# Gated linear attention with causal experts on one core: scores from split operands, the first half batch by chunks, a compact state, eight PSUM banks and a hinted branch

## The chip, the cores and the metric

The kernel runs on 1 core of a Trainium2 chip. The metric is the device time in microseconds (us); before the change the median of 3 runs is 330.34 us (329.6 to 331.68). An execution taken by the profiler took 328.62 us, and its span, from the first to the last instruction, is 326.9 us. The engines are named as in the profile: PE is TensorE, PEld its weight loads, DVE is VectorE, ACT is ScalarE, POOL is GpSimd, SP is SyncE, which issues every DMA.

## What is computed

A linear attention with a decaying state gives y, and y goes through four causal attention heads ("experts") of which each token takes two.

```python
for t in range(S):                       # B, H, S, D = 4, 8, 768, 48
    state = alpha[:, :, t, :, None] * state + np.einsum('bhd,bhe->bhde', k[:, :, t], v[:, :, t])
    y[:, :, t] = np.einsum('bhd,bhde->bhe', q[:, :, t], state)
...
logits = x @ w_gate                      # x: y with the heads side by side, 768 x 384 for each batch
... w: softmax of the two largest logits of a token, 0 for the others
for e in range(E):                       # 4 experts, 64 wide
    q, k, v = x @ wq[e], x @ wk[e], x @ wv[e]
    scores = np.where(causal, -1e9, scale * (q @ k.transpose(0, 2, 1)))
    a = softmax(scores)
    out += w[e] * (a @ v @ wo[e])
```

## The kernel before

**Units and chunks.** The time axis is cut into 24 chunks of 128 tokens (6 for each of 4 batches). Three chunks make a unit, a half batch, of which there are 8. A chunk's linear attention ("gla") does this: `prep_r` and `prep_c` (L417, L442) run two scans over alpha on DVE and scale q and k with the results; `gla_a` (L474) forms k times q on PE into two PSUM tiles, which go to SBUF masked (one by DVE, L489; the other by ACT and then POOL, L492 and L496); `gla_t` transposes k (L507); `gla_u` (L516) multiplies k by v for the state, and brings the state S forward (the decay at a chunk's end is `ev`) in two halves, on DVE (L544) and then POOL (L547); `gla_y` (L571) forms y, which is split into a rounded part `xh` (ACT, L581) and the remainder `xl` (DVE, L585). `check` squares the scans into `acc` (L471), from which the end of the kernel learns whether the scans stayed in range.

**A unit's experts.** `front(u)` makes the projections of a whole unit: `proj` (L604) nine products xh·wh, xl·wh, xh·wl of 384 columns for q and k of each of two pairs of experts, `vproj` (L622) the same with 260 columns for v and the gate, and `gate` on DVE. q and k come out in plain fp32 (ACT, L609 and L612). `back(u)` then runs, for each pair and each of the unit's three row blocks i, `score` (two fp32 products q·k, one for each expert of the pair, on rows 0 to 63 and 64 to 127 of the array, L679; DVE adds the causal mask and takes the row's extreme in one instruction, L687; ACT takes the exponential, L696), `norm` (two small DVE instructions L708 and L709, then POOL scales the row block, L715), `transp` (PE transposes L733, ACT copies L747), `av` (L770) and `outp` (L796, ACT L801, and the DMA to the output, L803).

**What sets the order.** The program is written as steps (`op` of class `Plan`, L82) with an engine, costs and the tiles they read and write; `schedule` (L122) plays them through these costs and picks, for each engine, the step that can start first, and among those within 0.05 us the one that was written first. The result is a fixed order for each engine. `emit` issues it, and wherever the plan leaves PE idle for over 0.45 us in the first 45 us it adds filler products (`warm`, L979) into an eighth PSUM bank of their own; the plan has the other seven (`GB = 7`). How far units and chunks run ahead of each other is set by the `mix` weights. The first unit starts like this: three chunks one after the other, then the splits of the weights into a rounded part and a remainder (`wqk_l`, `wv_l`, `wo_l`), then `front(0)`.

**The end.** After the last step DVE counts the flags in `acc`, PE sums them (L989), DVE writes the sum `cnt` (L991), each engine loads it into a register (L992) and compares (L993): if any scan left its range, a long exact program runs, otherwise the engines jump over it to the end.

## Time and profile before

| what | value |
|---|---|
| median of 3 runs | 330.34 us |
| profiled execution, and its span | 328.62 us, 326.9 us |
| PE busy in the span | 317.0 us (97%) |
| DVE busy | 239.7 us (73%) |
| ACT busy | 214.3 us (66%) |
| POOL busy | 134.3 us (41%) |
| DMA read and written | 24.44 MB, 4.72 MB |

A PE matmul of fp32 operands is recorded as two passes, so 128 score products are 256 records. Matmuls overlap: a record's length holds the way through the array too, and what one costs in a stream is the distance to the next one's start. On DVE and ACT likewise each record is some 0.08 to 0.1 us longer than the distance between starts.

### The profile page before, as it was taken

Reading aid. Unit: us, or ns where it says so; the run is one execution under the profiler, and the core shown is the slowest. Engines: PE = TensorE matmul, PEld = TensorE weight load, DVE = VectorE, ACT = ScalarE, POOL = GpSimd, SP = SyncE. Lnnn points to the kernel's source line nnn. Section 1 sums busy time; section 2 is a strip of 40 time slices with the busy share of each in tenths; the row PEclk is TensorE's granted clock in tenths of the full one; section 3 lists DMA queues with packets and bytes.
Section 4 is the critical chain, followed back from the end, with each engine's and each line's share of the span. In section 5 each row is a group of like instructions: output and inputs, shape, how many; then the busy total and the mean of one; then the engine's idle time right before and its main releaser. Section 6 shows DMA issues by size and latency. Waiting matters only on the chain.

```text
span 326.9 us, 9547 instructions
## 1 busy us (share of the span) xinstructions
PE 317.0 (97%) x3715; PEld 265.0 (81%) x3715; DVE 239.7 (73%) x692; ACT 214.3 (66%) x543; POOL 134.3 (41%) x190
## 2 busy tenths in 40 slices
PE   8999999999999999999999999999999999999991
PEld 6879988879797897988888687988978786957690
DVE  6899999899999999989797780939359155195420
ACT  1464586759875595756659296856837658569750
POOL 4142267434473366814349071615315324236310
PEclk9999999999999999999999999999999999999996
DMA  6999355144323253234240610412000000100101
GB/s 193 281 269 244 88 145 154 30 135 145 106 83 111 72 164 116 93 100 121 59 138 26 172 37 1 119 50 88 0 26 26 26 0 2 49 27 7 67 24 60
DMA packets 13797, 29.85 MB, mean 91 GB/s; under 512 B 1616, under 2 KB 4912, under 8 KB 13744
## 3 DMA queue, kind: packets, MB, share of 16 engines
q1 hardware_dynamic: 13744, 29.16, 31.1%
q8 instruction: 31, 0.51, 0.7%
q14 instruction: 22, 0.18, 0.2%
HBM read 24.44 MB, written 4.72 MB: 89 GB/s over the span
## 4 chain that ended last, share of the span: by engine, by line
PE 92%; DVE 4%; POOL 1%; ACT 1%; issue 0%; POOLq 0%; ACTq 0%; DVEq 0%
PE g L604 15%; PE g L679 11%; PE g L571 11%; PE g L733 11%; PE g L770 10%; PE g L796 8%; PE g L622 8%; PE g L480 7%; PE pw L979 5%; PE g L525 3%; PE g L507 2%; DVE a L687 1%; POOL a L715 1%; DVE al L451 0%; DVE qk L455 0%
## 5 line engine op out<-in xcount | busy, mean ns | idle before, releaser
L715 POOL TENSOR_SCALAR a<-a,cf,gw 128x128 f32<-128x128 f32 (+5 forms) x96 | 88.7, 936 | 62.9 <-DVE cf L709 43.1
L696 ACT ACTIVATE a<-a,mx 128x128 f32<-128x128 f32 (+5 forms) x96 | 63.3, 662 | 17.6 <-DVE mx L687 17.4
L687 DVE CUSTOM_DVE_ANT_0 a<-g,cm 128x384 f32<-128x384 f32 (+3 forms) x96 | 47.1, 529 | 5.1 <-PE g L679 4.8
L747 ACT ACTIVATE at<-g 128x512 f32<-128x512 f32 (+3 forms) x124 | 48.4, 465 | 0.9 <-PE g L733 0.7
L733 PE MATMUL g<-ident,a 128*128 128x128 f32 x336 | 46.3, 275 | 0.5 <-DVE mx L687 0.2
L679 PE MATMUL g<-k,q 64*128 64x256 f32 (+3 forms) x256 | 43.8, 454 | 0.0
L733 PEld LDWEIGHTS g<-ident,a 128*128 128x128 f32 x336 | 38.1, 141 | 5.2 <-POOL a L715 2.3
L770 PE MATMUL g<-at,vg 128*64 128x384 f32 (+2 forms) x324 | 39.5, 391 | 0.0
L770 PEld LDWEIGHTS g<-at,vg 128*64 128x64 f32 x324 | 20.9, 137 | 18.3 <-issue 14.4
L547 POOL TENSOR_TENSOR S<-st,ev 48x192 f32<-48x192 f32 x32 | 20.4, 637 | 36.1 <-DVE st L544 35.1
L604 PE MATMUL g<-xh,wqk_h 128*128 128x384 f32 x96 | 34.4, 358 | 0.1
L571 PE MATMUL g<-ms,vt 128*32 128x128 f32 x768 | 33.2, 275 | 0.1
L604 PE MATMUL g<-xl,wqk_h 128*128 128x384 f32 x96 | 32.4, 338 | 0.0
L604 PE MATMUL g<-xh,wqk_l 128*128 128x384 f32 x96 | 32.4, 338 | 0.0
L428 DVE TENSOR_TENSOR_SCAN al<-al,d1r 112x516 f32<-112x516 f32 (+1 forms) x25 | 30.2, 1212 | 2.4 <-DMA al<-in_al_dram 2.4
L679 PEld LDWEIGHTS g<-k,q 64*128 64x128 f32 x256 | 23.9, 186 | 9.4 <-issue 4.7
L451 DVE TENSOR_TENSOR_SCAN al<-al,d1c 112x516 f32<-112x516 f32 (+1 forms) x25 | 30.6, 1223 | 0.5
L496 POOL TENSOR_SCALAR_AFFINE_SELECT ms<-ms 128x512 f32<-128x512 f32 x24 | 16.2, 675 | 33.2 <-ACT ms L492 32.6
L471 ACT ACTIVATE al<-al 112x1033 f32<-112x1033 f32 x24 | 25.8, 1075 | 1.7 <-DVE qk L459 1.2
L480 PEld LDWEIGHTS g<-qk 48*128 48x128 f32 x384 | 24.2, 187 | 3.2 <-issue 1.2
L480 PE MATMUL g<-qk 48*128 48x128 f32 x384 | 26.2, 278 | 0.0
L571 PEld LDWEIGHTS g<-ms,vt 128*32 128x32 f32 x768 | 20.6, 109 | 5.3 <-issue 2.3
(91 smaller groups left out, 624.2 us busy)
## 6 DMA issues: line engine op xcount, KB each, us to landing
qk<-in_qk_dram SPq DMA_DIRECT2D x23, 448.0 KB, 4.3
vt<-in_v_dram SPq DMA_DIRECT2D x24, 256.0 KB, 4.4
al<-in_al_dram SPq DMA_DIRECT2D x23, 226.2 KB, 2.7
out_dram<-ot SPq DMA_DIRECT2D x24, 192.0 KB, 1.9
at<-in_wqk_dram SPq DMA_DIRECT2D x1, 768.0 KB, 11.1
qk<-in_qk_dram SPq DMA_DIRECT2D x2, 224.0 KB, 3.2
at<-in_wvg_dram SPq DMA_DIRECT2D x1, 390.0 KB, 10.6
at<-in_wo_dram SPq DMA_DIRECT2D x1, 384.0 KB, 12.7
```

The costliest lines, as they stand in the source:

```text
L428: V.tensor_tensor_scan(backwards(al[0:P, AW + c0 - 1:AW + c1 - 1]), backwards(al[0:P, c0:c1]), d1r[0:P, sl].rearrange("p a w -> p (a w)"), ...
L451: V.tensor_tensor_scan(c, c, T(("d1c", n))[0:P, sl].rearrange("p a w -> p (a w)"), 0.0, OP.mult, OP.max)
L480: PE.matmul(T(("pa", n, s))[:, C * p:C * p + C], t[r:r + D, p, C:2 * C], t[r:r + D, p, 0:C], start=True, stop=True, tile_position=(r, 0))
L571: PE.matmul(py[32 * j:32 * j + 32, k], l, r, start=(i == 0), stop=(i == len(parts) - 1), tile_position=(0, 32 * j))
L604: PE.matmul(pj[:, :W3], w[:, kt, cs], x[:, kt, :], start=(i == 0), stop=(i == 8))
L679: PE.matmul(T(sk[e])[:, :w], q[r, ts], k[r, c0:c1], start=True, stop=True, tile_position=(64 * e, 0))
L687: V.tensor_tensor_reduce(T(ak[e])[:, c0:c1], T(sk[e])[:, :w], cm[:, m0:m0 + w], -1.0, mx[:, 0:1] if x else BIG, OP.add, OP.min, accum_out= ...
L696: A.activation(a[:, 0:n], a[:, 0:n], AF.Exp, bias=T(mk)[:, e, len(pieces) - 1:len(pieces)], scale=-1.0, accum_out=T(("sm", u))[:, ix:ix + 1])
L715: G.tensor_scalar(a[:, 0:n], a[:, 0:n], T(ck_)[:, e:e + 1], T(("gw", u))[:, i, eg:eg + 1], op0=OP.mult, op1=OP.mult)
L733: PE.transpose(pt[:, 128 * (j - j0):128 * (j - j0) + 128], a[:, 128 * j:128 * j + 128], ident)
L747: A.activation(dst, src, AF.Copy)
L770: PE.matmul(py[64 * e:64 * e + 64, lo:n1], v[:, j % 3, 64 * eg:64 * eg + 64], at[e][:, at_off(j) + lo:at_off(j) + n1], start=(j == 0), sto ...
```

## The change

- **Scores.** q and k are kept split, like x: a rounded part (ACT) and the remainder (a DVE subtraction, new: `split`), both of type fp32r, which PE takes in one pass. A score is then three products, q1·k1 + q1·k2 + q2·k1, for each of the two experts, in alternation.
- **First unit.** `projp` makes q and k of unit 0 for one chunk at a time, 18 products of 128 columns for a pair; `vproj` follows each chunk; the splits of the weights stand ahead of chunk 1; scores of pair 0 start after each chunk. SP's first loads are ordered anew, the weights ahead of v of chunk 1. The chunk numbered 5 is loaded twice, once by the new loop and once by `chunk(3)`.
- **State.** The state is kept as C, 112 partitions x 192; one DVE and one POOL instruction bring it forward in place of two and two; ACT copies both halves into S (two new instructions a chunk, 40 in all).
- **Chunks 0 to 2** have both masked tiles made by ACT and POOL, not DVE. One d1c buffer in place of two; three buffers for q (twice the size) in place of four.
- **Eight banks.** The plan has all eight PSUM banks; fillers go to the eighth until the plan first takes it.
- **Order.** A table of 552 turns (`TURN`) replaces "written first" as the choice among steps that could start about together.
- **The end.** The count of flags (`verdict`) is a step ahead of the last unit; each engine gets a branch prefetch hint some 9 us before the planned end; the range test of the loaded value is left out.

```diff
-DMA_RATE = 220.0
+DMA_RATE = 250.0
...
-GB = 7
-MS_DVE = 0
+GB = 8
+HINT = 9.0
+TURN = (
+    5, 17, 3, 30, 13, 72, 1, 4, 117, 15, 6, 154, 142, 59, 65, 61, 8, 93, 84, 223, 180, 68, 56, 97, 123, 29, 52, 102,
...
+MS_ACT = 3
...
-                        t, i = min(c, key=lambda x: x[1])
+                        t, i = min(c, key=lambda x: rank[x[1]])
...
+                warming = warming and all(self.slot_of[k] != GB - 1 for k in o["new"] if self.kinds[k[0]] == "g")
...
-                if o["start"] < WARM_UNTIL and gap > WARM_GAP:
+                if warming and gap > WARM_GAP:
...
-        "q": slots("q", 4, [128, W3]),
-        "k": slots("k", 3, [128, S]),
+        "q": slots("q", QB, [128, 2, W3], F32R),
+        "k": slots("k", 3, [128, 2, S], F32R),
...
+            if c == 0:
+                op("V", 0.36, 0.37, lambda T: V.tensor_tensor(T(("C", n + 1))[0:P], pu(T), e(T), OP.mult),
+                   r=whole(("pu", n)) + ev, w=whole(("C", n + 1)))
+            else:
+                op("V", 0.36, 0.37, lambda T: V.tensor_tensor(T(("C", n + 1))[0:P], pu(T), T(("C", n))[0:P], OP.add),
+                   r=whole(("pu", n), ("C", n)), w=whole(("C", n + 1)))
+                op("G", 0.52, 0.53, lambda T: G.tensor_tensor(T(("C", n + 1))[0:P], T(("C", n + 1))[0:P], e(T), OP.mult),
+                   r=ev, w=whole(("C", n + 1)))
...
+                op("A", 0.21, 0.3, lambda T, rows=rows, cols=cols: A.activation(
+                    T(("S", n + 1))[rows, :, cols], T(("C", n + 1))[rows], AF.Copy),
+                   r=whole(("C", n + 1), ("S0",)), w=[(("S", n + 1), s)])
...
+        def split(src, c0, n, key, d0, part):
+            cs, ds = slice(c0, c0 + n), slice(d0, d0 + n)
+            op("A", *act(n), lambda T: A.activation(T(key)[:, 0, ds], T(src)[:, cs], AF.Copy),
+               r=whole(src), w=[(key, (0, part))])
+            op("V", *vec(n), lambda T: V.tensor_tensor(T(key)[:, 1, ds], T(src)[:, cs], T(key)[:, 0, ds].bitcast(F32),
+                                                       OP.subtract),
+               r=[(src, None), (key, (0, part))], w=[(key, (1, part))])
...
-                    for e in (0, 1):
-                        r = slice(64 * e, 64 * e + 64)
-                        PE.matmul(T(sk[e])[:, :w], q[r, ts], k[r, c0:c1], start=True, stop=True,
-                                  tile_position=(64 * e, 0))
-                occ = 2 * (0.008 + w / 1200)
...
+                    for m, (x, y) in enumerate(((0, 0), (0, 1), (1, 0))):
+                        for e in (0, 1):
+                            r = slice(64 * e, 64 * e + 64)
+                            PE.matmul(T(sk[e])[:, :w], q[r, x, ts], k[r, y, c0:c1], start=(m == 0), stop=(m == 2),
+                                      tile_position=(64 * e, 0))
+                occ = 3 * (0.013 + w / 2400 if w > 128 else N128)
...
+                for which in (0, 1):
+                    col = slice(256 * which + 128 * pair, 256 * which + 128 * pair + 128)
+                    m = 0
+                    for kt in range(3):
+                        for w, x in ((wqk_h, xh), (wqk_h, xl), (wqk_l, xh)):
+                            PE.matmul(pj[:, 128 * which:128 * which + 128], w[:, kt, col], x[:, kt, cs],
+                                      start=(m == 0), stop=(m == 8))
...
+            vproj(0, n)
...
+            for pair in (0, 1):
+                projp(0, pair, n)
+            if n:
+                score(0, 0, n - 1)
+            loads(n + 3)
...
+    for e, x in ((PE, "PE"), (V, "V"), (A, "A"), (G, "G"), (SY, "S")):
+        with tc.issue_after(pl.anchor[x].ins):
+            tc.mark_branch_hint_location("exact", "LikelyTaken", [e.engine])
```

What the new order does is seen on three queues. First PE, around the first score; before (L480 is `gla_a`, L679 the scores of q and k, g are PSUM banks):

```order
L480 MATMUL g_69<-qk_74 128x128
L679 MATMUL g_65<-k_104,q_100 128x128
L679 MATMUL g_64<-k_104,q_100 128x128
L679 MATMUL g_68<-k_104,q_100 128x256
L679 MATMUL g_67<-k_104,q_100 128x256
L679 MATMUL g_66<-k_104,q_100 128x384
L679 MATMUL g_69<-k_104,q_100 128x384
L571 MATMUL g_63<-ms_91,vt_81 32x128 x4
```

and now (L869 is `projp`, L555 `gla_t` of chunk 2, L730 the scores):

```order
L869 MATMUL g_67<-xh_96,wqk_h 128x128
L869 MATMUL g_67<-xl_98,wqk_h 128x128
L869 MATMUL g_67<-xh_96,wqk_l 128x128
L555 MATMUL g_66<-ident,qk_77 128x112 x4
L730 MATMUL g_68<-k_103,q_100 128x128
L730 MATMUL g_69<-k_103,q_100 128x128
L730 MATMUL g_68<-k_103,q_100 128x128
L730 MATMUL g_69<-k_103,q_100 128x128
L730 MATMUL g_68<-k_103,q_100 128x128
L730 MATMUL g_69<-k_103,q_100 128x128
L528 MATMUL g_70<-qk_77 128x128
```

A score of one width is now six products into two banks, in turns, where it was two; and the first one stands ahead of `gla_a` of chunk 2, where it stood behind that of chunks 3 and 4.

Second, DVE in the start; before, from chunk 2's second scan on (L455 and L459 scale k and q, al is alpha, at holds the unsplit weights):

```order
L451 SCALAR_TENSOR_TENSOR al_2_72<-al_2_72,d1c_0_86 112x516
L455 TENSOR_TENSOR qk_2_76<-qk_2_76,al_2_72 112x4x128
L459 TENSOR_TENSOR qk_2_76<-qk_2_76,al_2_72 112x4x128
L373 SCALAR_TENSOR_TENSOR wqk_l_155<-at_0_137,wqk_h_154 128x3x256
L585 TENSOR_TENSOR xl_0_98<-g_1_64,xh_0_96 128x3x128
L377 TENSOR_TENSOR wqk_l_155<-at_0_137,wqk_h_154 128x3x256
L489 TENSOR_TENSOR ms_0_90<-g_4_67,mask_149 128x512
L544 TENSOR_TENSOR st_1_93<-g_0_63,S_1_95 48x192
L428 SCALAR_TENSOR_TENSOR al_3_73<-al_3_73,d1r_147 112x516
L544 TENSOR_TENSOR st_1_93<-g_0_63,S_1_95 48x192
L432 RECIPROCAL d1c_1_87<-al_3_73 112x4
L381 TENSOR_TENSOR wv_l_157<-at_1_138,wv_h_156 128x780
```

and now (L662 is the remainder of q or k):

```order
L471 RECIPROCAL d1c_0_87<-al_2_73 112x4
L421 TENSOR_TENSOR wv_l_158<-at_1_137,wv_h_157 128x780
L490 SCALAR_TENSOR_TENSOR al_2_73<-al_2_73,d1c_0_87 112x516
L413 SCALAR_TENSOR_TENSOR wqk_l_156<-at_0_136,wqk_h_155 128x3x256
L633 TENSOR_TENSOR xl_0_98<-g_7_70,xh_0_96 128x3x128
L588 TENSOR_TENSOR C_1_93<-g_0_63,C_0_92 112x192
L417 TENSOR_TENSOR wqk_l_156<-at_0_136,wqk_h_155 128x3x256
L424 TENSOR_TENSOR wo_l_160<-at_1_137,wo_h_159 128x768
L494 TENSOR_TENSOR qk_2_77<-qk_2_77,al_2_73 112x4x128
L498 TENSOR_TENSOR qk_2_77<-qk_2_77,al_2_73 112x4x128
L662 TENSOR_TENSOR q_0_100<-g_2_65,q_0_100 128x128
L662 TENSOR_TENSOR k_0_103<-g_2_65,k_0_103 128x128
```

The remainders of the weights moved ahead of chunk 2's scaling, the masked tile of chunk 2 left this queue, and the remainders of q and k came into it.

Third, SP at the end; before (ISA x2 is the range test):

```order
L803 DMA out_0_dram<-ot_0_145 128x384
L803 DMA out_0_dram<-ot_1_146 128x384
L992 TENSOR_LOAD cnt_3889
L992 ISA x2
L993 COMPARE_AND_BRANCH
```

and now:

```order
L1186 BRANCH_PREFETCH_HINT
L856 DMA out_0_dram<-ot_1_145 128x384
L856 DMA out_0_dram<-ot_0_144 128x384
L856 DMA out_0_dram<-ot_1_145 128x384
L1087 TENSOR_LOAD cnt_153
L1088 COMPARE_AND_BRANCH
```

The range test is gone, and the hint stands three output DMAs ahead of the branch; PE, DVE, ACT and POOL have one too.

## Rows read from the trace of the kernel before

**Rows 1.** The page: the span, the busy time of the engines with its share and the count of instructions, and two lines of the 40 slices (busy tenths of DVE, granted clock of PE in tenths).

```profile
span 326.9 us, 9547 instructions
PE 317.0 (97%) x3715; PEld 265.0 (81%) x3715; DVE 239.7 (73%) x692; ACT 214.3 (66%) x543; POOL 134.3 (41%) x190
DVE  6899999899999999989797780939359155195420
PEclk9999999999999999999999999999999999999996
```

**Rows 2.** Busy time by stretch of the span (from:to, its length, then busy us and instructions of PE, PEld, DVE, ACT and POOL, granted clock, DMA share, GB/s).

```profile
27.20:45.40 18.20, 18.20 (x261) 16.93 (x262) 17.33 (x46) 10.75 (x27) 4.54 (x9) 1.00 0.50 121
45.40:138.50 93.10, 92.67 (x1154) 79.81 (x1155) 88.93 (x227) 68.18 (x178) 52.84 (x63) 1.00 0.39 116
138.50:319.50 181.00, 180.38 (x1935) 147.34 (x1933) 110.61 (x381) 122.76 (x319) 67.22 (x92) 1.00 0.18 53
319.50:326.90 7.40, 0.08 (x2) 0.00 (x0) 0.14 (x1) 0.49 (x1) 0.00 (x0) 0.66 0.20 66
```

**Rows 3.** The chain that ended last, in order of time (start, length, what): the end of the start.

```profile
25.65 1.52 PE pw L979 x13
27.18 1.09 PE g L622 x9
```

**Rows 4.** Groups of instructions by line and shape (records, then busy us, mean ns of one, idle time ahead of them): the scores by width, products in the one-pass type, fillers, and weight loads of 128 and 32 columns.

```profile
L679 PE MATMUL g<-k,q 64*128 64x512 f32 x64 | 17.5, 604 | 0.0
L679 PE MATMUL g<-k,q 64*128 64x256 f32 x96 | 15.5, 389 | 0.0
L679 PE MATMUL g<-k,q 64*128 64x384 f32 x64 | 13.9, 492 | 0.0
L679 PE MATMUL g<-k,q 64*128 64x128 f32 x32 | 3.5, 274 | 0.0
L604 PE MATMUL g<-xh,wqk_l 128*128 128x384 f32 x96 | 32.4, 338 | 0.0
L979 PE MATMUL pw<-d1r 128*128 128x256 bf16 x117 | 15.9, 290 | 1.6 <-POOL d1r L388 1.6
L604 PEld LDWEIGHTS g<-xh,wqk_l 128*128 128x128 f32 x96 | 18.0, 188 | 0.0
L571 PEld LDWEIGHTS g<-ms,vt 128*32 128x32 f32 x768 | 20.6, 109 | 5.3 <-issue 2.3 <-DVE mx L687 1.7 <-DVE cf L709 0.3
```

**Rows 5.** PE in order of time (start, length, count): a score of 512 columns and what follows it; one of 128 columns and what follows it; two one-pass products of 260 columns; two of 384.

```profile
246.42 1.03 PE L679 MATMUL g<-k,q 64*128 64x512 f32 x4
247.28 1.06 PE L480 MATMUL g<-qk 48*128 48x128 f32 x16
...
130.92 0.39 PE L679 MATMUL g<-k,q 64*128 64x128 f32 x4
131.15 1.06 PE L480 MATMUL g<-qk 48*128 48x128 f32 x16
...
27.62 0.28 PE L622 MATMUL g<-wv_h,xl 128*128 128x260 f32 x1
27.74 0.28 PE L622 MATMUL g<-wv_h,xh 128*128 128x260 f32 x1
...
300.59 0.34 PE L796 MATMUL g<-wo_h,yh 128*128 128x384 f32 x1
300.77 0.34 PE L796 MATMUL g<-wo_l,yh 128*128 128x384 f32 x1
```

**Rows 6.** The start in order of time: the first scan, then the remainders of the weights on DVE, and ACT's rounding of wqk.

```profile
3.03 0.70 DVE L428 TENSOR_TENSOR_SCAN al<-al,d1r 112x258 f32<-112x258 f32 x1 [1.01 <-DMA al<-in_al_dram]
...
17.63 0.84 ACT L364 ACTIVATE wqk_h<-at 128x768 fp32r<-128x768 f32 x1 [0.67 <-DMA at<-in_wqk_dram]
...
22.30 0.95 DVE L377 TENSOR_TENSOR wqk_l<-at,wqk_h 128x768 fp32r<-128x768 f32 x1
...
33.24 0.67 DVE L455 TENSOR_TENSOR qk<-qk,al 112x512 f32<-112x512 f32 x1
33.82 0.69 DVE L459 TENSOR_TENSOR qk<-qk,al 112x512 f32<-112x512 f32 x1
```

**Rows 7.** Groups by line and shape, as in rows 4, of DVE: remainders of 384 and of 128 columns, and the state.

```profile
L585 DVE TENSOR_TENSOR xl<-g,xh 128x384 fp32r<-128x384 f32 x24 | 13.2, 549 | 10.4 <-ACT xh L581 10.2
L544 DVE TENSOR_TENSOR st<-g,S 48x192 f32<-48x192 f32 x32 | 11.3, 353 | 5.2 <-PE g L525 3.9 <-POOL S L547 0.4 <-ACT at L747 0.4
L781 DVE TENSOR_TENSOR yl<-g,yh 128x128 fp32r<-128x128 f32 x3 | 0.9, 292 | 2.3 <-ACT yh L779 2.2
```

**Rows 8.** The end: the last output DMAs, and the sequencers' instructions of two lines (count, shortest/median/longest ns, first and last start).

```profile
319.01 1.38 SPq L803 DMA_DIRECT2D out_dram<-ot  x2
...
L993 SPq EVENT_SEMAPHORE  x8: 17/17/17, 324.4 to 324.9; - x8
...
L993 PEldq COMPARE_BRANCH  x1: 4322/4322/4322, 320.6 to 320.6; - x1
L993 SPq COMPARE_BRANCH  x1: 45/45/45, 321.3 to 321.3; - x1
...
L1091 SPq EVENT_SEMAPHORE  x10: 17/28/28, 325.0 to 326.8; - x10
```

**Rows 9.** The page's list of DMA issues (count, KB each, median us from issue to landing): the output.

```profile
out_dram<-ot SPq DMA_DIRECT2D x24, 192.0 KB, 1.9
```

More of the change, by code (lines that the diff above doesn't have):

```diff
@@ L245, in emit @@
             if warm is not None and o["eng"] == "PE":
+                warming = warming and all(self.slot_of[k] != GB - 1 for k in o["new"] if self.kinds[k[0]] == "g")
                 gap = o["start"] - pe
[L247 removed]
+                if warming and gap > WARM_GAP:
                     warm(int(gap / WARM_MM * 0.8))
                 pe = o["start"] + o["occ"]
[L250 removed]
+            x = o["fn"](self.tile)
+            if x is not None and o["start"] < self.end - HINT:
+                self.anchor[o["eng"]] = x
 @with_exitstack
@@ L472, in check, with verdict, f @@
             op("A", 1.05, 1.15, f, r=whole(("acc",)), w=whole(("al", n)) + whole(("acc", n)))
+        def verdict():
+            def f(T):
+                V.tensor_scalar(okm[0:P, 1:], acc[0:P], SAFE, None, op0=OP.is_le)
+                V.tensor_reduce(okm[0:P, 0:1], okm[0:P, 1:], axis=AX.X, op=OP.add)
+            op("V", 0.25, 0.3, f, r=whole(*[("acc", n) for n in range(NG)]), w=whole(("okm",)))
+            op("PE", 0.05, 0.2, lambda T: PE.matmul(T(("pk", 0))[0:1, 0:1], okm[0:P, 0:1], ones[0:P], start=True, stop=True),
+               pe="pk", r=whole(("okm",), ("lm",)), w=whole(("pk", 0)))
+            op("V", 0.09, 0.15, lambda T: V.tensor_copy(cnt, T(("pk", 0))[0:1, 0:1]), r=whole(("pk", 0)), w=whole(("cnt",)))
         def gla_a(n):
@@ L816, in front, with back @@
                     yield
-        def back(u):
+        def back(u, made=0):
             tail = u == NU - 1
@@ L823, in back @@
                 if k < len(seq):
-                    score(u, *seq[k])
+                    if k >= made:
+                        score(u, *seq[k])
                     norm(u, *seq[k])
@@ L896, in build @@
         constants()
+        load_al(1)
         load_v(0)
-        load_al(1)
         load_q(1)
+        wload(1)
         constants2()
         load_v(1)
-        for p in (0, 2):
-            prep_r(0, p, 2)
-            prep_c(0, p, 2)
-        loads(2)
-        gla_a(0)
-        gla_t(0)
-        check(0)
-        wload(0)
-        gla_y(0)
-        run(chunk(1))
-        wload(1)
-        constants3()
-        run(chunk(2))
-        split_hi(0)
-        split_lo(0)
-        split_lo(1)
-        split_hi(1)
-        split_lo(2)
+        load_al(2)
+        wload(0)
+        load_q(2)
+        load_v(2)
+        for n in range(HALF):
+            if n == 0:
+                for p in (0, 2):
+                    prep_r(0, p, 2)
+                    prep_c(0, p, 2)
+            else:
+                prep_r(n)
+                gla_u(n - 1)
+                prep_c(n)
+            gla_a(n)
+            gla_t(n)
+            gla_y(n)
+            if n == 0:
+                split_hi(1)
+                split_lo(2)
+            vproj(0, n)
+            if n == 0:
+                split_hi(0)
+                split_lo(0)
+                split_lo(1)
+                constants3()
+            for pair in (0, 1):
[3 more added lines that the diff above has]
+            loads(n + 3)
+        check(0)
+        check(1)
+        check(2)
         split_lo(3)
         half = lambda h: gla(h) if h < NU else None
-        b, g = chain(front(0), back(0)), half(1)
+        gate(0)
+        b, g = back(0, 2), half(1)
         mix((b, MIX_BACK0), (g, MIX_GLA0), until=g)
```

137 lines of the change are left out of this document (71 added, 66 removed), and 23 rows, old and new, of the table TURN.

## The prediction

> **What bounds the kernel now.** I read the page first: PE is busy 97% of the span; DVE's slices are at 8 and 9 through the first half and lower after it [rows 1]. Then the chain in order of time: it runs through fillers up to the first v product of the experts at 27.18 us [rows 3]. There are 117 fillers [rows 4]; at 256 columns, 0.12 us each by the products of 260 columns [rows 5], they are some 13 us of work that no result needs. Then the stretches after it [rows 2]. From 27.2 to 138.5 us PE is full (110.9 of 111.3 us) and DVE nearly so: 17.3 of 18.2 us, then 88.9 of 93.1 us [rows 2]. From 138.5 to 319.5 us PE alone is full, and DVE works 110.6 of 181 us. The last 7.4 us hold no work at all. The clock is granted in full throughout [rows 1]. So a saving on PE counts where DVE does not hold it up, DVE's own additions are nearly free after 138.5 us and not before, and the empty end counts in full.
>
> **Scores.** A score of 512 columns (both experts) takes 0.86 us of PE's queue, start to next start, and one of 128 takes 0.23 us [rows 5]; in between I go in a straight line: 0.44 and 0.65 us for 256 and 384. By the records (four for each score of two experts) there are 8, 24, 16 and 16 scores of 128, 256, 384 and 512 columns [rows 4]: 8 x 0.23 + 24 x 0.44 + 16 x 0.65 + 16 x 0.86 = 36.6 us. Now each is three steps of two one-pass products. A one-pass product costs 0.12 us at 260 columns and 0.18 at 384 [rows 5], that is its columns at 2.4 GHz plus 0.013 us: 0.226, 0.173 and 0.120 us at 512, 384 and 256. Do the two experts' products run side by side? No one-pass products on half the array stand in this trace. The two-pass ones do run so: a record of 512 columns lasts 604 ns, against 338 ns for 384 one-pass columns, of which 160 are columns and 178 the way through [rows 4]; 604 - 178 = 426 ns, and four such start within 860 ns [rows 5], so two run at a time. I take the same for one pass. A step of 128 columns would cost 0.066 us by its columns; but each product loads 128 columns of weights. Loads last 188 ns for 128 columns and 109 for 32 [rows 4], so 0.82 ns a column, 105 ns for 128, and I see no product here that was shorter than its load. I take 0.105 for it, which is nearer to what was seen, and keep 0.066 for the range. Sum: 8 x 0.32 + 24 x 0.36 + 16 x 0.52 + 16 x 0.68 = 30.4 us. **Scores: -6.2 us** (-7.2 with narrow steps at 0.066).
>
> The Trainium skill, "TensorE: Matmul & The Clock Gate", section "Back-to-back issue gap", gives 81 ns for a product of 128 columns in a stream of loads and products, between my two values; no run here shows it. By it the narrow steps below would cost 2.6 us less than in my sum.
>
> **The start.** Before, the projections waited for wqk_l, whose second half DVE began at 22.30 us [rows 6]. Now it stands ahead of chunk 2's scaling. Adding DVE's new queue from its first scan at 3.03 us [rows 6] with the start-to-start distances (0.6 us for 512 columns, as 33.24 to 33.82 [rows 6], hence about 0.08 less than each record's length; 1.15 for a scan): chunk 0 4.8 us, chunk 1 and its state 5.0, chunk 2's scans with wv_l, wqk_l, the first xl and C 4.9, and about 1 us of waits, as before: wqk_l is done at 18.7 us and not 23.2. The weights come from DMA earlier (they pass v of chunk 1 on SP's queue), so ACT's rounding, at 17.63 us before, isn't late. The first q and k products start 8.2 us sooner than at 26.9 and, with the v product made before them (1.1 us), PE is ahead by 9.3; but work that before lay ahead of them now lies behind: y of chunks 1 and 2 and the rest of chunk 2, 4.5 us. Left: 4.8. Against it, q and k of unit 0 are 108 products of 128 columns at 0.105 = 11.3 us in place of 36 at 0.176 = 6.3: +5.0 (+0.8 at 0.066). And PE waits for DVE in between, since the remainder of chunk 1's x stands behind two scans of chunk 3: about 1 us (3.5 if the narrow products are short, since then the wait is only longer). **Start: +1 us** (-0.5 to +2.5). The 54 fillers fewer are no gain beyond this. Two things cost nothing by my reading: the second load of chunk 5 (0.93 MB) goes where the DMA share falls to 0.5 and less [rows 2], and the one d1c buffer, written by the DVE instruction just ahead of its reader. Without cover the load would be 3.5 us of a full DMA queue, ahead of chunk 6.
>
> **VectorE.** Added: 12 remainders of 128 and 28 of 384 columns, 0.21 and 0.47 us (records of 292 and 549 ns [rows 7] less 0.08). Removed: half of the 40 state instructions (0.28 us each, record 353), three masked tiles (0.6), one memset. Over the kernel +8 us, most of it late where DVE has 70 us free. Before the end of unit 1 (138.5 us) it is 12 x 0.21 + 12 x 0.47 - 8 x 0.28 - 2 x 0.6 - 0.5 = +4.3 us, where 4.2 us were free [rows 2]. Some of it will reach PE, some fills waits: **+1.5 us** (0 to +5.5). ACT gets 40 copies into S of about 0.25 us and three masked tiles, 12 us on an engine with 112 us free; POOL loses 16 state instructions.
>
> **Order and banks.** PE shows no idle time to take after 27.2 us [rows 2]; what a new order and an eighth bank can take are waits too short to show as idle, inside the matmuls' overlap. Changes between row, column and full tiling are as many as before (76 and 78 along PE's order). I put a small gain here: **-1 us** (0 to -4).
>
> **The end.** The last two output DMAs are issued from 319.0 to 320.4 us. SP then loads and tests cnt, branches at 321.3, and only at 324.4 executes the next instruction; PE's branch lasts 4.32 us [rows 8]. These are waits for the target's code, which no engine holds. From 324.4 to the end at 326.8 SP's two strings of semaphore instructions and the last barrier take 2.4 us [rows 8]. If the hint brings the code, SP stands at its branch some 0.6 us after its last issue, at 321.0, and starts the strings there; the last output lands 1.9 us after its issue at 320.1 [rows 9], about 322.0, in the midst of the first string, and what is left of the 2.4 us ends about 323.8. **-3.0 us**; without an effect of the hint only the test goes, -0.4.
>
> **Sum:** 326.9 - 6.2 + 1 + 1.5 - 1 - 3.0 = 319.2 us of span. The profiled execution had 1.7 us around its span, which makes 320.9; its 328.62 us lie 1.7 us under the median shown, within the runs' spread of 2.1 us, so I leave it at **321 us**, 2.8% under the median.
>
> **Rivals.** (A) *The one-pass products on half arrays run one after the other.* Against it stand the two-pass records above; for it, that no such product is in the trace. Then the 192 steps cost twice, 2 x 29.4 = 58.8 us in place of 30.4: 349 us, slower. It turns the sign once a quarter of the side-by-side is lost (7.7 of 28.4 us). (B) *VectorE is the bound up to 138.5 us.* For it: 95% busy there, and a remainder of q and k now stands between a projection and its scores; against it, that the PE queue was full all the same. Then the 4.3 us and some more land on PE, +5.5 in place of +1.5: 325 us. (C) *The hint changes nothing*, if the engines still fetch at the branch: +2.6, 323.5 us. (D) *Narrow products go by their columns, and the new order takes more of the waits:* -1.0 at the scores, -1 at the start and -3 at waits: 316 us.
>
> **How the numbers follow.** My forecast 0.38, A 0.07, B 0.15, C 0.15, D 0.25. Range 312 to 328: from D with all its bounds to B with the hint failing as well; A is left out, and a little at either end. For this kernel about 1% (3.3 us, so 327.0 and 333.6) can be told from no change. Faster: the forecast, C, D, nearly, and half of B or a little more, less what I may have missed: 0.79. Same: 0.12. Slower: A and a little: 0.09.
>
> **What would show it.** Scores: the 512-column score's six records within 0.7 us (A: 1.3). Start: first `projp` near 18.7 us, its products 0.105 us apart or 0.066; PE from 45 to 138 us full, with DVE above 95% (B: holes on PE before it). End: SP's semaphore instructions right behind the branch, and under 4.7 us from the last product to the end of the span. The prediction is wrong if the granted clock falls in the hole that I expect on PE ahead of the first projections, from about 14 to 17 us, where no filler is left: at 1.2 GHz the first products would cost up to 2 us more; or if the new order meets a late DMA or bank that the plan did not have.

## The result, and the profile after

The changed kernel is faster: the ratio to the kernel before is 0.974 (95% interval 0.970 to 0.979). Its four executions took 321.4, 322.4, 327.8 and 328.5 us (median 325.1), four of the kernel before 329.2 to 331.7 (median 330.0). In the two long ones the mean granted clock was 0.975; the ratio leaves them out, and run 2 shows where in the program the clock fell. The profiled execution is the one of 321.4 us, with a span of 319.7; predicted were 321 us and 319.2 us of span. The number was right, but most of its terms were not: that their misses cancel is luck.

The page of the changed kernel, as [rows 1]:

```profile
span 319.7 us, 9830 instructions
PE 309.8 (97%) x3861; PEld 275.3 (86%) x3861; DVE 242.2 (76%) x708; ACT 229.1 (72%) x594; POOL 120.2 (38%) x177
DVE  5999879999999999989999978447674364269430
PEclk9999999999999999999999999999999999999998
```

Busy time by stretch, as [rows 2]:

```profile
27.20:45.40 18.20, 18.20 (x280) 17.34 (x284) 15.63 (x39) 10.70 (x30) 3.84 (x7) 1.00 0.51 153
45.40:138.50 93.10, 93.10 (x1308) 83.76 (x1301) 88.55 (x231) 71.52 (x183) 38.21 (x53) 1.00 0.41 121
138.50:315.50 177.00, 174.75 (x1990) 154.09 (x1988) 115.79 (x402) 131.80 (x350) 66.26 (x91) 1.00 0.17 55
315.50:319.70 4.20, 0.00 (x0) 0.00 (x0) 0.00 (x0) 0.00 (x0) 0.00 (x0) 0.62 0.03 11
```

PE is as full as before and DVE works 88.55 of 93.1 us, where it worked 88.93: by busy time nothing has changed up to 138.5 us. PE has 1308 records there, before 1154, but that is no measure of more work: a score has six records now where it had four, and most of the other additions are short products of the chunks' y and state. What PE got done is counted under the experiments.

DVE from the start to 138.5 us, before and now:

```profile
0.00:138.50 138.50, 136.52 (x1782) 117.67 (x1783) 128.93 (x311) 91.03 (x223) 67.05 (x99) 1.00 0.51 143
```
```profile
0.00:138.50 138.50, 135.08 (x1874) 121.23 (x1875) 126.41 (x307) 97.28 (x245) 53.91 (x87) 1.00 0.52 152
```

It is busy 126.4 us there, 2.5 less than before, although the 24 remainders stand in it.

Groups by line and shape, as [rows 4]: the scores, one of the narrow products, and the fillers.

```profile
L730 PE MATMUL g<-k,q 64*128 64x512 f32 x96 | 14.5, 407 | 0.0
L730 PE MATMUL g<-k,q 64*128 64x256 f32 x144 | 13.2, 287 | 0.0
L730 PE MATMUL g<-k,q 64*128 64x384 f32 x96 | 11.9, 347 | 0.0
L730 PE MATMUL g<-k,q 64*128 64x128 f32 x48 | 4.1, 274 | 0.0
L869 PE MATMUL g<-xl,wqk_h 128*128 128x128 f32 x36 | 10.0, 277 | 0.0
L1078 PE MATMUL g<-d1r 128*128 128x256 bf16 x63 | 9.5, 320 | 1.5 <-POOL d1r L428 1.5
```

In order of time, as [rows 5] and [rows 6]: a score of 512 columns, one of 256 right behind it and what follows them; one of 128; two narrow products; then the second half of wqk_l on DVE and the first v product.

```profile
99.86 0.94 PE L730 MATMUL g<-k,q 64*128 64x512 f32 x6
100.64 0.52 PE L730 MATMUL g<-k,q 64*128 64x256 f32 x6
101.09 0.32 PE L573 MATMUL g<-vt,kt 128*64 128x48 f32 x4
...
24.01 0.55 PE L730 MATMUL g<-k,q 64*128 64x128 f32 x6
24.40 0.77 PE L528 MATMUL g<-qk 48*128 48x128 f32 x10
...
23.29 0.28 PE L869 MATMUL g<-xl,wqk_h 128*128 128x128 f32 x1
23.40 0.27 PE L869 MATMUL g<-xh,wqk_l 128*128 128x128 f32 x1
...
18.73 0.95 DVE L417 TENSOR_TENSOR wqk_l<-at,wqk_h 128x768 fp32r<-128x768 f32 x1
...
18.01 0.40 PE L672 MATMUL g<-wv_h,xh 128*128 128x260 f32 x1 [1.25 <-ACT xh L629]
```

This score of 512 columns takes 0.78 us and the one of 256 takes 0.45, to the next start. Within the first, the three steps of two products start at 99.86, 100.18 and 100.41 us: 0.23 us for 512 columns of both experts, so the two products run side by side, and some 0.09 us more for the first step behind another kind of product. From the start of each score's records to the next start on PE, summed, the scores take 34.9 us; before it was 41.1. By width, 512 to 128 columns, a score takes 0.76, 0.60, 0.43 and 0.36 us in the mean; before 0.91, 0.73, 0.51 and 0.35. The narrow products stand 0.111 us apart.

The end, as [rows 8]: PE's last output product before the change; then, of the changed kernel, that product, the last two output DMAs, two branches and what follows SP's, and two of the hints.

```profile
319.13 0.33 PE L796 MATMUL g<-wo_h,yl 128*128 128x384 f32 x1
```
```profile
312.92 0.34 PE L848 MATMUL g<-wo_h,yl 128*128 128x384 f32 x1
...
312.81 1.38 SPq L856 DMA_DIRECT2D out_dram<-ot  x2
...
L1088 SPq EVENT_SEMAPHORE  x8: 17/17/17, 317.8 to 318.3; - x8
...
L1088 PEldq COMPARE_BRANCH  x1: 408/408/408, 312.2 to 312.2; - x1
...
L1088 SPq COMPARE_BRANCH  x1: 70/70/70, 314.8 to 314.8; - x1
...
L1186 SPq BRANCH_PREFETCH_HINT  x1: 50/50/50, 300.0 to 300.0; - x1
...
L1186 PEldq BRANCH_PREFETCH_HINT  x1: 45/45/45, 305.5 to 305.5; - x1
```

PE's branch is short now (0.41 us, before 4.32 [rows 8]). SP still stands 3.0 us between its branch and its next instruction. From the start of the last output product to the end of the span it is 6.8 us; before, that product started at 319.13 us, 7.8 us ahead of the end. So 6.2 of the span's 7.2 us were gained ahead of the last output product and 1.0 behind it; the sum had 4.7 and 3.0.

### The profile page after: what moved, and what is told of

Same layout as the page of the kernel before. It is cut to its first block, busy times and chain, and to the rows that moved or that the text cites. A ratio compares the mean times of both kernels' runs of the same rounds, so it can differ in the third digit from the quotient of the medians.

```text
span 319.7 us, 9830 instructions
## 1 busy us (share of the span) xinstructions
PE 309.8 (97%) x3861; PEld 275.3 (86%) x3861; DVE 242.2 (76%) x708; ACT 229.1 (72%) x594; POOL 120.2 (38%) x177
## 5 line engine op out<-in xcount | busy, mean ns | idle before, releaser
L767 POOL TENSOR_SCALAR a<-a,cf,gw 128x128 f32<-128x128 f32 (+5 forms) x96 | 77.9, 826 | 64.9 <-DVE cf L761 23.1
L730 PE MATMUL g<-k,q 64*128 64x256 f32 (+3 forms) x384 | 37.0, 331 | 0.0
L544 POOL TENSOR_SCALAR_AFFINE_SELECT ms<-ms 128x512 f32<-128x512 f32 x27 | 21.8, 815 | 38.6 <-ACT ms L540 38.3
L822 PEld LDWEIGHTS g<-at,vg 128*64 128x64 f32 x324 | 22.4, 137 | 15.9 <-issue 10.8
L730 PEld LDWEIGHTS g<-k,q 64*128 64x128 f32 x384 | 29.5, 185 | 3.1 <-issue 0.5
L590 POOL TENSOR_TENSOR C<-C,ev 112x192 f32<-112x192 f32 x16 | 11.0, 688 | 50.9 <-DVE C L588 49.6
L652 PE MATMUL g<-xh,wqk_h 128*128 128x384 f32 x84 | 29.9, 356 | 0.0
L652 PE MATMUL g<-xh,wqk_l 128*128 128x384 f32 x84 | 28.3, 336 | 0.0
L652 PE MATMUL g<-xl,wqk_h 128*128 128x384 f32 x84 | 28.2, 336 | 0.0
L619 PE MATMUL g<-qk,S 112*32 112x128 f32 x480 | 24.2, 272 | 0.0
```

Of the source, the lines that this page charges most:

```text
L619: PE.matmul(py[32 * j:32 * j + 32, k], l, r, start=(i == 0), stop=(i == len(parts) - 1), tile_position=(0, 32 * j))
L652: PE.matmul(pj[:, :W3], w[:, kt, cs], x[:, kt, :], start=(i == 0), stop=(i == 8))
L730: PE.matmul(T(sk[e])[:, :w], q[r, x, ts], k[r, y, c0:c1], start=(m == 0), stop=(m == 2), tile_position=(64 * e, 0))
L767: G.tensor_scalar(a[:, 0:n], a[:, 0:n], T(ck_)[:, e:e + 1], T(("gw", u))[:, i, eg:eg + 1], op0=OP.mult, op1=OP.mult)
L822: PE.matmul(py[64 * e:64 * e + 64, lo:n1], v[:, j % 3, 64 * eg:64 * eg + 64], at[e][:, at_off(j) + lo:at_off(j) + n1], start=(j == 0), sto ...
```

## The experiments

To see where time goes although PE is always "busy", I count the work that PE has started: each product of a result at one pace for its kind in all kernels (scores at their new pace, a narrow product as a third of a wide one), fillers not at all. These are the times (us) at which a share of it was started, in the profiled executions, one for each kernel. Differences of under 1 us between two rows can be the execution alone: that of run 5 is the shortest of its six, 0.8 us under their median.

| kernel | 2% | 15% | 30% | 50% | 90% | all |
|---|---|---|---|---|---|---|
| before | 19.3 | 61.9 | 107.1 | 166.1 | 286.9 | 319.1 |
| changed | 19.9 | 65.0 | 109.1 | 167.5 | 283.5 | 312.9 |
| 4, remainders twice | 20.2 | 65.7 | 111.9 | 171.4 | 288.0 | 317.5 |
| 5, fillers and early hints | 19.3 | 64.4 | 108.4 | 166.8 | 282.9 | 312.3 |
| 6, no table | 22.0 | 68.6 | 113.8 | 172.5 | 290.4 | 321.4 |
| 7, wide first unit | 22.8 | 64.0 | 108.6 | 169.8 | 293.8 | 323.9 |
| 8, before, split scores | 19.5 | 62.5 | 108.4 | 168.9 | 287.9 | 319.4 |
| 10, as 8, no remainders | 19.4 | 63.6 | 109.4 | 169.4 | 287.4 | 318.8 |

The short waits themselves can be estimated too. For each start on PE from 62 to 312 us I take its distance from the start before it, less the lower quartile of that distance for the same two kinds of product in that execution, and sum it where another engine's semaphore had only just ended a wait. That gives 4.2 us before, 0.9 in the changed kernel and 1.1 in run 5; 1.7 in run 9, 4.3 in run 4, 4.2 in run 6, 7.6 in run 8 and 5.7 in run 10. Of the 4.2 us, 1.6 are waits for the row extremes on DVE (`mx`), 1.0 for POOL's scaling and 0.7 for the old state instructions.

The theory after the result: the scores gave what was predicted, the hint reached only PE, and the order made up for it. The rival, as in the prediction: VectorE decides up to 138 us.

**1. Without the hints.**

```diff
-    for e, x in ((PE, "PE"), (V, "V"), (A, "A"), (G, "G"), (SY, "S")):
-        with tc.issue_after(pl.anchor[x].ins):
-            tc.mark_branch_hint_location("exact", "LikelyTaken", [e.engine])
```

> The changed kernel with the five hints left out and nothing else. Readings of the changed kernel's trace: after their branches ACT goes on 3.1 us later, SP 2.9 us and DVE 2.8 us later, POOL 2.6, as SP did before the change (3.05 us); only PE's branch is short (0.41 us, where it was 4.32). Theory (the hints reached PE alone, and PE is not last): the end of the span does not move, at most 0.3 us, and PE's branch is 4 us long again but over before SP's semaphores end. Rival (the hints brought the 0.9 us by which the end, from the last output product on, got shorter): 0.9 us longer than the changed kernel, 322.3 us of execution in place of 321.4.

Two of the four executions had the low clock; the two with a clock over 0.99 took 321.9 and 322.5 us, as with the hints. PE's branch is long again, and SP's semaphores start 2.7 us behind its branch:

```profile
L1085 PEldq COMPARE_BRANCH  x1: 3517/3517/3517, 312.5 to 312.5; - x1
...
L1085 SPq COMPARE_BRANCH  x1: 45/45/45, 315.5 to 315.5; - x1
L1085 SPq EVENT_SEMAPHORE  x8: 17/17/17, 318.2 to 318.7; - x8
```

PE was over at 316.1 us, ahead of SP. From the start of the last output product (313.15 us) to the end it is 6.9 us, 0.2 more than with the hints. So they brought at most 0.2 of the 1.0 us; the rest is there without them, with the flags counted earlier and the range test gone.

**2. Early hints.**

```diff
-HINT = 9.0
+HINT = {"PE": 9.0, "V": 60.0, "A": 75.0, "G": 110.0, "S": 270.0}
-            if x is not None and o["start"] < self.end - HINT:
+            if x is not None and o["start"] < self.end - HINT[o["eng"]]:
```

> The changed kernel with the hints of four engines set earlier: DVE 60 us, ACT 75, POOL 110 and SP 270 us ahead of the planned end in place of 9 us. In the trace each of these engines fetches its next 8 KB of code when it is 40 to 65 instructions into a block of 128; in the changed kernel none of the four did so between its hint and its branch, and no fetch followed their hints. Theory A (a hint on these engines takes effect only with the engine's next fetch): now a fetch stands behind each hint, SP goes on within 0.3 us of its branch, and the end of the span comes 1.2 to 2.9 us sooner, about 317.5 us of span. Theory B (these engines have no room for a hinted block beside the two in sequence): no gain at the end, 319.7 us, or longer if a block in sequence is pushed out on the way, by about 3 us for each on a busy engine.

The ratio is 0.971 (0.966 to 0.975). SP and ACT go on 0.5 us after their branches; the rows stand with run 5, which repeats it. Theory A holds for the gain; its fetch behind each hint I did not find. The queue that serves these engines moved fewer packets, not more (the page's list of queues: packets, MB, share; the changed kernel, then run 5):

```profile
q14 instruction: 22, 0.18, 0.2%
```
```profile
q14 instruction: 18, 0.15, 0.2%
```

The four packets that are missing are of the end: from 305 us on there are four in place of eight, and from the start to 300 us 14 in both. In which earlier packet the hinted code comes stays open. The Trainium skill, "Runtime: NRT & Kernel Launch", section "Instruction fetch mechanics", says that a taken branch to a block outside the two held must fetch it first; the 2.6 to 3.1 us here fit that. It names no hint.

This run also caught the low clock: two of its six executions had it, the profiled one among them. Stretches of run 2, then of the changed kernel's profiled execution:

```profile
12.00:18.00 6.00, 4.62 (x80) 3.70 (x77) 5.97 (x8) 5.95 (x12) 1.65 (x3) 1.00 1.03 321
...
19.20:32.50 13.30, 13.30 (x107) 12.60 (x110) 7.33 (x16) 4.72 (x14) 4.78 (x6) 0.50 0.57 147
```
```profile
12.00:18.00 6.00, 4.62 (x82) 3.77 (x80) 5.42 (x8) 5.67 (x11) 1.47 (x3) 1.00 1.03 326
...
19.20:32.50 13.30, 13.30 (x180) 12.65 (x179) 12.41 (x26) 7.86 (x22) 6.34 (x8) 1.00 0.89 229
```

Both have a hole on PE ahead of the first projections, 1.4 us of idle time in all. In one the clock fell to its lower level (0.50, 1.2 GHz) for over 13 us and PE had 107 records in place of 180; in the other it stayed.

**3. Scores by two passes again,** order kept, remainders left out.

```diff
-            op("V", *vec(n), lambda T: V.tensor_tensor(T(key)[:, 1, ds], T(src)[:, cs], T(key)[:, 0, ds].bitcast(F32),
-                                                       OP.subtract),
+            op("V", *vec(n), lambda T: None,
...
-                    for m, (x, y) in enumerate(((0, 0), (0, 1), (1, 0))):
...
+                        PE.matmul(T(sk[e])[:, :w], q[r, 0, ts].bitcast(F32), k[r, 0, c0:c1].bitcast(F32), start=True, stop=True,
+                                  tile_position=(64 * e, 0))
```

> The changed kernel, its order kept, with the scores taken back: q and k are not split (the 40 remainders on VectorE are left out) and each score is one fp32 product of two passes for each expert. The records of the scores took 41.0 us of PE before and 35.0 us now. Theory (PE alone is the bound, VectorE's remainders cost nothing in this order): 6 us longer, 327.4 us of execution. Rival (the remainders cost the +1.5 us that the prediction put on them, or more): 4.5 us longer or less, 326 us.

Three of four executions had the low clock. The other took 326.9 us, 5 us over the changed kernel (321.4 and 322.4). One execution can't tell 6 from 4.5; run 9 asks for the remainders by themselves.

**4. Remainders computed twice,** order kept.

```diff
-            op("V", *vec(n), lambda T: V.tensor_tensor(T(key)[:, 1, ds], T(src)[:, cs], T(key)[:, 0, ds].bitcast(F32),
-                                                       OP.subtract),
+            op("V", *vec(n), lambda T: [V.tensor_tensor(T(key)[:, 1, ds], T(src)[:, cs], T(key)[:, 0, ds].bitcast(F32),
+                                                        OP.subtract) for _ in (0, 1)][1],
```

> The changed kernel, its order kept, with each of the 40 remainders of q and k computed twice on VectorE (12 of 128 and 28 of 384 columns again, 0.21 and 0.47 us each: 8.2 us more before 138.5 us, where VectorE has 4.5 us free, and 7.5 us more later, where it is free). Theory (VectorE is not the bound, its free time is where PE needs none): under 1.5 us longer. As the prediction priced it (a third of the added time reaches PE): 2.5 to 3 us longer. Rival B of the prediction (VectorE bounds the kernel up to 138.5 us): 4 us longer or more, with holes on PE before 138 us.

One of four executions had the low clock. The others took 326.0, 326.0 and 326.4 us: 4.2 us longer, and PE has holes:

```profile
45.40:138.50 93.10, 91.16 (x1299) 81.11 (x1291) 90.68 (x241) 69.96 (x178) 33.28 (x49) 1.00 0.41 119
```

So 8.2 us more than the change put on VectorE would cost half of it. That says what the next microseconds cost, not what the first did: for that see run 9.

**5. Fillers in the hole, and early hints.**

```diff
                 if warming and gap > WARM_GAP:
                     warm(int(gap / WARM_MM * 0.8))
+                elif gap > 1.0 and o["start"] < 45.0:
+                    for key in [key for key in o["new"] if self.kinds[key[0]] == "g"][:1]:
+                        warm(int(gap / WARM_MM * 0.6), self.tile(key))
...
-            PE.matmul(pools["g"][GB - 1][:, 0:256], zb[:, 0:128], zb, start=True, stop=True)
+            PE.matmul((bank or pools["g"][GB - 1])[:, 0:256], zb[:, 0:128], zb, start=True, stop=True)
```

> The kernel with the early hints, and ten filler products (256 columns, into the bank of the product behind them) ahead of the first v product, where PE idled 1.25 us in the changed kernel's profile. In that kernel's executions with a low granted clock the rows show PE idle in parts between 15.6 and 18.2 us, the clock at 0.53 from 19 to 20 us and at 0.50 from there to 32 us, and the execution 5 to 6 us longer; the kernel before had none in eleven executions. Theory (the hole lets the clock fall): with the fillers all executions stay at a granted clock over 0.99 and within 1% of each other, about 320 us. Rival (the low clock comes from outside the program): as before, a third to a half of the executions are 5 us longer. At the end: DVE, ACT and SP go on 0.5 us after their branches, the span ends 1.2 to 2.9 us sooner than in the changed kernel.

All six executions took 319.2 to 321.0 us with a clock of 0.996 or more; the ratio is 0.970 (0.967 to 0.974). The hole, in order of time:

```profile
15.87 1.27 PE L1081 MATMUL g<-d1r 128*128 128x256 bf16 x10
17.37 0.39 PE L675 MATMUL g<-wv_h,xh 128*128 128x260 f32 x1 [0.23 <-ACT xh L632]
```

Over all runs, the kernels of the new start without these fillers (changed, 1 to 4) had the low clock in 10 of 22 executions, those with them (5, 6, 7, 9, 11, 12) in 0 of 40 below 0.98, and the kernel before in 0 of 63. So the hole has to do with the fall; whether it comes in one execution is chance. But idle time alone doesn't decide it: the profiled executions of runs 7 and 9 have holes of 2.0 us there, with fillers behind them, and kept the clock. Nor were the two groups on one chip: runs 1 to 4 had one, runs 5 to 12 three others. So it isn't excluded that the chip plays a part, though the kernel before kept its clock on all of them. The Trainium skill, "TensorE: Matmul & The Clock Gate", Part 1, says that the moment of a clock change differs between executions of one kernel.

At the end:

```profile
312.25 0.34 PE L851 MATMUL g<-wo_h,yl 128*128 128x384 f32 x1
...
L1091 ACTq COMPARE_BRANCH  x1: 68/68/68, 313.5 to 313.5; - x1
...
L1091 SPq COMPARE_BRANCH  x1: 70/70/70, 315.0 to 315.0; - x1
L1091 SPq EVENT_SEMAPHORE  x8: 17/17/17, 315.5 to 316.1; - x8
...
L1091 ACTq EVENT_SEMAPHORE  x1: 17/17/17, 313.9 to 313.9; - x1
```

From the last output product's start to the end it is now 5.2 us (span 317.5), 1.6 less than in the changed kernel.

**6. Without the table of turns** (on run 5).

```diff
-    pl.schedule(turn=TURN)
+    pl.schedule()
```

> The kernel with early hints and fillers, without the table of turns (the plan takes the steps in the order in which they are written). As the prediction priced order and banks together (-1 us): at most 1 us longer than with the table. If the start costs +1 us as predicted, the order must hold what is left of the sum (the last output product came 6.2 us sooner; the scores -6.0, VectorE about +1.1): 2.3 us longer. Rival (the order is worth nothing, the start costs nothing): the same time within 0.5 us.

328.7 us, ratio 0.996 (0.993 to 0.998): 8.6 us longer than run 5, more than any of the three expectations. By the table above 2.7 us are lost by the first 2% of the work, 5.4 by 30%, 7.5 by 90% and 9.1 at the end. No single wait on PE from 60 us on is over 0.5 us there. Of the 4.9 us lost after 15%, the estimate of the short waits has 3.1 (4.2 us, run 5 1.1).

**7. Wide q and k products in the first unit** (on run 5): `projp` left out, `proj(0, pair, which)` behind the third chunk, the scores of unit 0 waiting for whole q and k.

```diff
-            for pair in (0, 1):
-                projp(0, pair, n)
-            if n:
-                score(0, 0, n - 1)
...
+                for pair in (0, 1):
+                    for which in (0, 1):
+                        pl.group -= which
+                        proj(0, pair, which)
...
```

> The kernel with early hints and fillers, its first unit's q and k projected in 36 products of 384 columns behind all three chunks, in place of 108 of 128 columns chunk by chunk. The narrow products measured 0.111 us apart, 12.0 us in all, against 6.3 us for the wide ones: 5.7 us of PE saved. Theory (as in the prediction: starting early is worth about what the narrow products cost): within 1.5 us of the kernel with the narrow ones, with PE idle ahead of the first projections instead. Rival 1 (the narrow products are a loss): 3 us shorter or more. Rival 2 (the early start is worth more than they cost): 2 us longer or more.

331.1 us, ratio 1.004 (1.002 to 1.007), 11 us over run 5: by the number that is rival 2. But at 15% and 30% of the work it stands where run 5 does (64.0 and 108.6, there 64.4 and 108.4): as far as the start goes, the early start is worth what the narrow products cost, as the theory said. The 11 us are lost from there on, 3 by half of the work and 11 by 90%. In the profiled execution some 5 of these (3.2 and half of 3.4) fall at one place, where PE waits 3.2 us for POOL's scaling, POOL having waited for DVE's `cf`, and then has the lower clock for 3.4 us:

```profile
273.58 1.71 PE L788 MATMUL g<-ident,a 128*128 128x128 f32 x7 [3.22 <-POOL a L770]
```
```profile
273.70:277.10 3.40, 3.40 (x17) 2.78 (x17) 1.74 (x4) 1.77 (x6) 3.40 (x6) 0.50 0.00 0
```

The four longest of its ten executions have a mean clock of 0.984 to 0.989, the others of 0.990 to 0.995. The plan has another order with a table made for the narrow products, so the run doesn't say what a wide start with a table of its own would take.

**8. The kernel before with split scores alone.**

```diff
-                        PE.matmul(T(sk[e])[:, :w], q[r, ts], k[r, c0:c1], start=True, stop=True,
-                                  tile_position=(64 * e, 0))
+                    for m, (x, y) in enumerate(((0, 0), (0, 1), (1, 0))):
...
+                            PE.matmul(T(sk[e])[:, :w], q[r, x, ts], k[r, y, c0:c1], start=(m == 0), stop=(m == 2),
+                                      tile_position=(64 * e, 0))
```

> The kernel before with the scores' part alone: q and k split, each score three steps of two one-pass products, one d1c buffer and three q buffers to make room; start, order, banks, state and end as before. Theory (scores -6.0 us on PE; 16 remainders of 384 columns, 7.5 us, fall before 138 us, where VectorE had 4.2 us free, so about 3.3 us come back): 2.5 to 3.5 us shorter than before, 327 us. Rival (VectorE's work is hidden): 6 us shorter, 324 us.

329.3 us, ratio 0.997 (0.995 to 1.000): 0.9 us of the 6. Neither expectation. The short waits on PE grew from 4.2 to 7.6 us, by the estimate above.

**9. Without remainders** (on run 5, order kept).

```diff
-            op("V", *vec(n), lambda T: V.tensor_tensor(T(key)[:, 1, ds], T(src)[:, cs], T(key)[:, 0, ds].bitcast(F32),
-                                                       OP.subtract),
+            op("V", *vec(n), lambda T: None,
```

> The kernel with early hints and fillers, its order kept, without the 40 remainders of q and k: their parts are set to zero once at the start by ACT, the three products of each score are made as before. Left out: the remainders, so the scores are those of rounded q and k. VectorE has 15.7 us less, 8.2 us of it before 138 us. The doubled remainders cost 4.1 us. If VectorE costs the path half of what it works up to 138 us on both sides: 4 us shorter, 316 us. As the prediction priced the additions, a third: 1.5 to 2.7 us shorter. If the remainders only used up time that was free: within 0.5 us of 320 us.

320.8 us, ratio 0.971 (0.968 to 0.973), run 5 has 0.970: nothing. DVE works less from 45 to 138 us (84.96 us, in the changed kernel 88.55), and PE is no faster:

```profile
45.40:138.50 93.10, 92.69 (x1317) 83.67 (x1310) 84.96 (x220) 71.68 (x182) 38.59 (x52) 1.00 0.42 121
```

In this order the remainders cost nothing. With run 3 that puts the scores at about 5 us of the path, from one execution of run 3.

**10. As run 8, without remainders** (the same edit).

> The kernel before with split scores, without the remainders of q and k (28 of 384 and their like, set to zero once at the start by ACT; the scores are those of rounded q and k). With the remainders it was only 0.9 us shorter than before, though PE saves 6 us on the scores. Theory (the remainders on VectorE ate the rest, since VectorE had only 4 us free before 138 us): 4 us shorter or more than with them, 324 to 325 us. Rival (the plan without a table puts the shorter scores where PE waits for something else): 328 us or more.

328.7 us, ratio 0.994 (0.992 to 0.996), by the ratios 1.2 us less than run 8, though the two intervals still touch. The rival holds: the remainders took about 1 us of the scores' 6, and nearly 4 are lost elsewhere. What PE waited for from 45 to 312 us, first before the change, then in this run (L740 are the transposes, L685 the scores; us in total, times, longest):

```profile
PE g L507 <- DVE st L544: 0.4, 1, 0.4
PE g L733 <- DVE mx L687: 0.2, 1, 0.2
```
```profile
PE g L740 <- POOL a L722: 0.8, 1, 0.8
PE g L685 <- DVE ms L495: 0.7, 2, 0.5
PE g L740 <- DVE mx L694: 0.6, 1, 0.6
PE g L740 <- DVE ms L495: 0.5, 1, 0.5
PE g L685 <- DVE mx L694: 0.4, 1, 0.4
```

So PE idles 2.4 us more, behind DVE's masked tiles and row extremes and POOL's scaling. That fits the order; but runs 8 and 10 also have one d1c buffer for two and three q buffers for four, and no run takes these apart from the order.

**11. Without the additions of 1e-9** (on run 5, order kept).

```diff
-                V.tensor_scalar(cf, T(("sm", u))[:, i0:i0 + 4:3], 1e-9, None, op0=OP.add)
-                V.reciprocal(cf, cf)
+                V.reciprocal(T(ck_), T(("sm", u))[:, i0:i0 + 4:3])
...
-                V.tensor_scalar(gm[:, 2], gm[:, 1], 1e-9, None, op0=OP.add)
-                V.reciprocal(gm[:, 3], gm[:, 2])
+                V.reciprocal(gm[:, 3], gm[:, 1])
```

> The kernel with early hints and fillers, its order kept, without the additions of 1e-9 to sums that are 1 or more, where they change nothing in fp32: 48 instructions of 0.21 us ahead of the reciprocals of the softmax sums and 8 of 0.36 us in the gate, 13 us of VectorE, about 4 us of them before 138 us. If VectorE costs the path half of what it works there: 2 us shorter, 318 us. As the prediction priced additions, a third: 1.3 us shorter. If VectorE is no bound in this order: the same, 320 us.

319.0 us, ratio 0.965 (0.963 to 0.967): 1 to 2 us less than run 5 (by the medians and by the ratios), and the best of all kernels here. Since run 9 took more work off VectorE for nothing, it is probably not their length that counts but their place, between each softmax sum and the scaling on POOL that waits for it; that is argued, not shown.

**12. Chunk 5 loaded once** (on run 11, order kept).

```diff
+                if n in made:
+                    for o in pl.ops[-3:]:
+                        o["fn"] = lambda T: None
+                made.add(n)
```

> The kernel of the run before (early hints, fillers, no small additions), its order kept, with chunk 5 loaded once: the second load of its alpha, q, k and v (0.93 MB) is left out. As the prediction read it (the load goes where the DMA queue has room): the same time within 0.3 us, 319 us. Rival (it stands in the full queue of the start, ahead of chunk 6): up to 3.5 us shorter, and chunk 6 lands sooner.

319.4 us, ratio 0.966 (0.964 to 0.969): the same. The second load is hidden.

## Why the prediction was right, step by step

- **Scores, -6.2 us: right, with both prices too low.** By the records the scores went from 41.1 to 34.9 us; the sum had 36.6 and 30.4. It took the shortest score of 512 and of 128 columns [rows 5] for the mean and left out what the first step behind another kind of product costs, in both kernels alike, so 4.5 us cancel in the difference. Rival A is out: 0.78 us for the 512-column score, over the 0.7 expected but far from 1.3.
- **Narrow products at 0.105 us: nearly right** (0.111), and rival D's 0.066 is out. The distance fits the price by the weight load (0.105); that the load sets it was not tested. The 81 ns that the Trainium skill gives ("TensorE: Matmul & The Clock Gate", "Back-to-back issue gap") are not reached here; the measurement decides.
- **Start, +1 us: too good.** wqk_l was done at 19.7 us, not 18.7, the first narrow product came at 19.55, and at 15% of its work PE is 3.1 us behind the kernel before, over the range of +2.5.
- **VectorE, +1.5 us: measured 0** (run 9). The +4.3 us up to 138.5 us under it (4.2 by its own terms) weren't there: DVE is busy 2.5 us less. The remainders came as counted, 12 narrow and 12 wide ones, but the sum took off 8 state instructions and 2 masked tiles, where the trace has 24 and 15 before and 13 and 11 now; and four row extremes are later. Rival B is out for this change, with little to spare: the remainders computed twice cost 4.2 us (run 4).
- **Order and banks, -1 us: the failed step, in kind.** From 15% of the work on the changed kernel gains 9.3 us on the kernel before, of which 5.9 are the scores: so 3.4 us for order, banks and compact state, within the step's range. The estimate of the short waits says the same by itself: 4.2 us before, 0.9 now. But it isn't a small term beside the others. The shorter scores alone gave 0.9 us (run 8), and the kernel of run 5 without its table is 8.6 us slower, 4.2 of them by 15% of the work (run 6). "PE shows no idle time to take" was read from busy time, and that hides the waits between products. What the eighth bank and the compact state are worth apart from the table wasn't tried and stays open.
- **The end, -3.0 us: -1.0.** The step "if the hint brings the code" failed: it brought PE's, whose branch is not the last, and not SP's. For the end rival C was right (run 1: at most 0.2 us by the hints). Set earlier, the hints give 1.6 us more (run 5).
- **The clock:** what "would make it wrong" happened in two of four executions, and cost some 6 us, not up to 2: in run 2's profiled execution the clock stayed low for over 13 us.

The misses cancel by luck: +2.1 (start), -1.5 (VectorE), -2.4 (order), +0.3 (scores: 0.3 of the 6.2 fall into the start), +2.0 (end). They make +0.5, and the span was 0.5 us over the prediction; since order is what was left of the whole, they had to add up to that.

## What to carry to other kernels

A full engine by busy time is no proof that it has no waits: count the work started by a given time, in both kernels, before you price an order at nothing. Where several engines are nearly full, a saving on one may not reach the end in an order made without it (run 8: 0.9 of 6 us); don't add the terms as if they were independent. A price read from one short place is not the mean: sum a kind's distances over the whole trace. Fillers that no result needs may still carry the clock: before they go, see what hole is left ahead of dense work.

## What had not been expected of the hardware

Branch hints 7 us (ACT, DVE), 15 us (SP) and 68 us (POOL) ahead of the branch did nothing, and hints 65 us (DVE), 75 us (ACT), 117 us (POOL) and 278 us (SP) ahead worked: 0.4 to 0.6 us from branch to next instruction in place of 2.8 to 3.2, on POOL 1.3 in place of 2.6. PE's worked 7 us ahead. What decides it isn't settled. With a hole of some 1.4 us on PE ahead of dense work the clock fell in 10 of 22 executions, for over 13 us in the one shown, and in none of 40 with the fillers, though two of those kernels show holes of 2.0 us. In run 7 it fell for 3.4 us behind a wait of 3.2 us.
